# Attention weight gradients from row-form dQ, dK, dV and O: DMA transposes in the backward recurrence instead of PE transposes in the gradient stage

## The chip, the cores and the metric

The kernel runs on one core of a Trainium2 chip. The time is the device time of one execution in microseconds. The engines are PE (TensorE, matmul; its weight loads are listed as PEld), DVE (VectorE), ACT (ScalarE), POOL (GpSimd) and SP (SyncE, which only issues DMAs here). DMAs issued by SP and ACT go to hardware queues, those issued by POOL to a software queue; all of them use the core's 16 DMA engines.

## The reference, cut to what matters

A forward and its backward pass. The block is a layernorm with modulation, a recurrent memory attention (A), another layernorm, and a gated FFN (B). The attention goes through 64 segments of 32 positions; each takes 8 memory rows that the segment before has produced, so the segments must run one after the other, forward in the forward pass and backward in the backward pass.

```python
for s in range(n_seg):                       # 64 segments
    h = concatenate([mem, x[:, s*32:(s+1)*32]])        # L = 40 rows of 512
    q = einsum('btd,dhe->bhte', h, Wq)       # 32 heads of 128; k and v alike
    scores = where(mask, einsum('bhqe,bhke->bhqk', q, k) * scale, -1e9)
    p = softmax(scores)
    o = einsum('bhqk,bhke->bhqe', p, v)
    o = einsum('bhte,hed->btd', o, Wo)
    mem = o[:, :8]; outs.append(o[:, 8:])
_out, _vjp = jax.vjp(f, x, mem0, Wq, Wk, Wv, Wo, w_gate, w_up, w_down, c, w_mod)
```

The outputs are the result and the gradients of the eleven inputs. The change is about four of them: dWq, dWk, dWv (512 x 32 x 128 each) and dWo (32 x 128 x 512), which are sums over all 64 x 40 rows: dWq = sum of h(row) times dQ(row), and dWo = sum of O(row) times dA(row).

## The kernel before, in words

All phases stand in one program. A scheduler orders the instructions of each engine by their dependences and adds the semaphore waits; each engine runs its list in order. A tile pool with `bufs=n` has n buffers of a tile; whoever writes a buffer again must wait for all who use it.

**Layout.** Heads are packed three to a group of 128 columns (3 x 40 = 120 used), 11 groups used of G = 12, so a tile of one segment is 128 x 1536. In the transposed form (QT, KT, VT, OT, dQT, dKT, dVT) the partitions are the 128 features of a head and a column is head-in-group times 40 plus row. In the row form (Ost, Pst, Qst, Kst) the partitions are head-in-group times 40 plus row and the columns of a group are the 128 features.

**phase2**, forward recurrence: per segment projections, scores, softmax, P times V (which gives Ost, in row form), transposes to OT, output projection. VT, OT, Pst, Qst and Kst are stored for the backward pass, 384 KB each, from POOL. Ost has one buffer and was not stored.

**phase3**: the FFN, forward and backward, then its weight gradients, meanwhile the transposes of the attention weights.

**phase4**, backward recurrence, segments 63 to 0. `get_loads` (line 983) fetches OT, VT, Pst, Qst, Kst of the next segment on SP's queue, with two buffers each. `dot_bank` makes dOT from dyT and Wo; `ds_part` the gradient of the scores; `grad_part` (line 1052) multiplies four groups into one PSUM bank and evacuates them into dVT, dKT or dQT; `dht` multiplies these by the weights, and the fold at the end gives the memory gradient that the next segment needs in dyT. `TailRows` collects the last 8 rows of each head with a POOL copy (`dh_tail`) and works them off in pieces over the following segments. At the segment's end POOL stores dVT, dKT and dQT (lines 1116 to 1118), and the memory rows DHA. dVT has two buffers, dKT and dQT one each.

**phase5**, from line 1121: `ln_tile` does the layernorm backward of 128 positions (16 in all, spread over the gradient groups), with small loads dhb on SP and an in-between product `pr` on POOL. `build_side_rows` loads h as `hrows` and dA as `dyrows`, with the row pair of a position on 2 x 64 partitions (two rows of each of 64 segments), 20 such steps. Then 44 groups (four tensors, 11 groups of heads): load `xt` (128 features x 64 segments x 128 columns, in runs of 256 B, alternately on SP and POOL); copy it to `xr` with the segments innermost (ACT two fifths, DVE the rest); transpose it on PE, 20 steps of up to three heads (`tpg`), evacuated into `rows` by DVE and ACT; and multiply `rows` with `hrows` (`gps`, 4 x 20 matmuls of up to 384 columns, line 1252) or with `dyrows` (`gps5o`, 20 of 512 columns a head, line 1262). The results are evacuated by ACT and stored by SP. dO comes last. The program ends with the gradients of the modulation.

## Time and profile before

| | us |
|---|---|
| median of 3 runs (lowest, highest) | 4122.3 (4118.8, 4124.72) |
| the profiled execution, its own time | 4126.9 |
| its span, first to last instruction | 4125.1 |
| PE busy (share of the span) | 3714.4 (90%) |
| PEld, DVE, ACT, POOL busy | 2687.0, 1960.2, 1619.0, 749.7 |
| DMA: moved, mean rate | 603.86 MB, 146 GB/s |
| window of the forward recurrence | 50 to 1380 and on to about 1474 |
| window of the FFN weight gradients | 1930 to 2123 |
| window of the backward recurrence | 2126 to 3249 |
| window of the attention weight gradients | 3304.4 to 4090.6 |

How to read it: the page gives for each engine its busy time in the span. A matmul is pipelined, so its listed duration (323 ns on average for the 384-column ones) is longer than the step from one to the next; pace is read from unbroken runs in the timeline. A group's line has its count, busy time, mean duration, the idle time of its engine just before it, and what ended that. A DMA's issue is on its queue's engine (SPq, ACTq, POOLq), its transfer on the 16 DMA engines; a queue's line has packets, MB and the share of the 16 engines' time.

### The profile page before, as it was taken

The numbers are of one execution on the slowest core, as the hardware profiler recorded it, in microseconds if no ns is written. First come the engines' busy times: TensorE is split into PE (matmuls) and PEld (weight loads), VectorE is DVE, ScalarE is ACT, GpSimd is POOL, SyncE is SP. The second block draws the span as 40 slices with busy tenths as digits, with TensorE's granted clock in tenths as the row PEclk, the third lists the DMA queues.
The fourth block names the chain that finished last, engine by engine and source line by source line (L and its number), as shares of the span: only waits on it lengthen the run. The fifth ranks groups of instructions, "written<-read, shape, count | busy, mean of one in ns | idle before, by whom it ended". The sixth has DMA issues, their size and how long they took to land. (4 is left out here: it accounts for less than half of the span.)

```text
span 4125.1 us, 147177 instructions
## 1 busy us (share of the span) xinstructions
PE 3714.4 (90%) x66669; PEld 2687.0 (65%) x66718; DVE 1960.2 (48%) x4005; ACT 1619.0 (39%) x2984; POOL 749.7 (18%) x1191
## 2 busy tenths in 40 slices
PE   2999999999999969996989999999999579998996
PEld 2778878888888855553556666666666356665653
DVE  3444444444444447763234444444444266565454
ACT  0344443444444435541223333333333155555553
POOL 2111111111111113331111111111111121111100
PEclk6999999999999989998999999999999799999998
DMA  6222232222222243335775555555555677776773
GB/s 226 94 106 94 98 106 97 97 105 105 92 96 102 102 142 126 122 104 165 227 226 190 190 190 190 189 178 187 184 190 182 153 169 168 159 165 135 146 146 114
DMA packets 558904, 603.86 MB, mean 146 GB/s; under 512 B 367082, under 2 KB 453370, under 8 KB 556612
## 3 DMA queue, kind: packets, MB, share of 16 engines
q1 hardware_dynamic: 489220, 316.00, 28.7%
q0 software_dynamic: 61200, 264.55, 18.4%
q10 hardware_dynamic: 7856, 13.89, 1.0%
q8 instruction: 521, 8.54, 0.9%
q14 instruction: 107, 0.88, 0.1%
HBM read 319.29 MB, written 275.02 MB: 144 GB/s over the span
## 5 line engine op out<-in xcount | busy, mean ns | idle before, releaser
L1252 PE MATMUL gps<-rows,hrows 128*128 128x384 bf16 (+1 forms) x2640 | 462.2, 323 | 11.2 <-ACT ot L61 8.8
L1252 PEld LDWEIGHTS <-hrows 128*128 128x128 bf16 x2640 | 253.7, 98 | 148.4 <-issue 13.6
L63 DVE COPY rows<-tpg 128x384 bf16<-128x384 bf16 (+1 forms) x616 | 199.8, 349 | 277.7 <-PE tpg L1245 150.2
L1245 PE MATMUL tpg<-ident,xr 128*128 128x128 bf16 x2560 | 225.1, 222 | 83.5 <-ACT xr L1238 49.2
L1245 PEld LDWEIGHTS <-xr 128*128 128x128 bf16 x2560 | 183.5, 99 | 142.4 <-ACT xr L1238 49.3
L1238 ACT ACTIVATE xr<-xt 128x3072 bf16<-128x3072 bf16 (+1 forms) x44 | 235.0, 5342 | 44.5 <-DMA dhb<-DHA 43.4
L393 PE MATMUL proj_ps<-hT,Wk 128*128 128x40 bf16 x8192 | 241.4, 181 | 0.3
L393 PE MATMUL proj_ps<-hT,Wq 128*128 128x40 bf16 x8192 | 241.5, 181 | 0.0
L393 PE MATMUL proj_ps<-hT,Wv 128*128 128x40 bf16 x8192 | 231.6, 179 | 0.1
L1025 PE MATMUL proj_ps<-dyT,WoT 128*128 128x40 bf16 x8192 | 228.4, 180 | 2.3 <-DMA dyT<-DAOT 2.3
L393 PEld LDWEIGHTS <-Wk 128*128 128x128 bf16 x8192 | 229.0, 97 | 0.5 <-issue 0.4
L393 PEld LDWEIGHTS <-Wq 128*128 128x128 bf16 x8192 | 229.2, 97 | 0.0
L1025 PEld LDWEIGHTS <-WoT 128*128 128x128 bf16 x8192 | 221.8, 96 | 2.8 <-issue 2.8
L393 PEld LDWEIGHTS <-Wv 128*128 128x128 bf16 x8192 | 222.5, 96 | 0.2 <-issue 0.2
L63 DVE CAST KT<-proj_ps 128x480 bf16<-128x480 f32 (+2 forms) x256 | 119.6, 488 | 191.9 <-PE proj_ps L393 186.0
L438 ACT ACTIVATE ET<-st_ps 128x480 bf16<-128x480 f32 x192 | 109.5, 570 | 226.9 <-PE st_ps L437 226.8
L1239 DVE COPY xr<-xt 128x4608 bf16<-128x4608 bf16 (+1 forms) x44 | 176.6, 4013 | 44.1 <-DMA dhb<-DHA 44.1
L61 ACT ACTIVATE rows<-tpg 128x384 bf16<-128x384 bf16 (+1 forms) x264 | 126.7, 480 | 159.2 <-PE tpg L1245 159.1
L61 ACT ACTIVATE QT<-proj_ps 128x480 bf16<-128x480 f32 (+2 forms) x256 | 104.9, 436 | 197.9 <-PE proj_ps L393 197.9
L539 DVE TENSOR_TENSOR Pst<-tps,rden 120x512 bf16<-120x512 bf16 x192 | 131.5, 686 | 100.0 <-PE tps L405 100.0
L61 ACT ACTIVATE dVT<-g_ps 128x512 bf16<-128x512 f32 x192 | 114.6, 597 | 135.7 <-PE g_ps L1056 135.7
L61 ACT ACTIVATE dQT<-g_ps 128x512 bf16<-128x512 f32 x192 | 114.6, 597 | 113.4 <-PE g_ps L1056 113.4
(332 smaller groups left out, 7725.2 us busy)
## 6 DMA issues: line engine op xcount, KB each, us to landing
VT<-VT POOLq DMA_DIRECT2D x64, 384.0 KB, 3.0
OT<-OT POOLq DMA_DIRECT2D x64, 384.0 KB, 2.6
PS<-Pst POOLq DMA_DIRECT2D x64, 384.0 KB, 3.3
QST<-Qst POOLq DMA_DIRECT2D x64, 384.0 KB, 2.7
KST<-Kst POOLq DMA_DIRECT2D x64, 384.0 KB, 2.9
OT_l<-OT SPq DMA_DIRECT2D x64, 384.0 KB
VT_l<-VT SPq DMA_DIRECT2D x64, 384.0 KB
Pst_l<-PS SPq DMA_DIRECT2D x64, 384.0 KB
```

Of the source, the lines that this page charges most:

```text
L61: return nc.scalar.activation(out, in_, AF.Copy)
L63: return nc.vector.tensor_copy(out, in_)
L393: nc.tensor.matmul(ps[:, g_, hl * L:(hl + 1) * L], lhsT=Ws[w][:, c, h * E:(h + 1) * E], rhs=hT[:, c, :], start=(c == 0), stop=(c == DC - 1))
L438: nc.scalar.activation(part3(ET, pi)[:, :, 0:120], st_ps[:, :, 0:120], AF.Exp, scale=cfg.scale)
L539: nc.vector.tensor_tensor(part3(Pst, pi)[0:120], ps[0:120, :, :], rden[:, pi * PG:(pi + 1) * PG].unsqueeze(2).to_broadcast([120, PG, 128]) ...
L1025: nc.tensor.matmul(ps[:, g_, hl * L:(hl + 1) * L], lhsT=WoT[:, c, h * E:(h + 1) * E], rhs=dyT[:, c, :], start=(c == 0), stop=(c == DC - 1))
L1238: nc.scalar.activation(xr[:, 0:cut, :], xt[:, :, 0:cut].rearrange("p s x -> p x s"), AF.Copy)
L1239: nc.vector.tensor_copy(xr[:, cut:W, :], xt[:, :, cut:W].rearrange("p s x -> p x s"))
L1245: nc.tensor.transpose(ps[0:KR, hl, :], xr[:, c0:c0 + 2, :].rearrange("p a s -> p (a s)"), self.ident[:, :])
L1252: nc.tensor.matmul(ps[:, 0:nh * E], lhsT=hrows[0:KR, tp_, c * 128:(c + 1) * 128], rhs=rows[0:KR, tp_, 0:nh * E], start=(tp_ == 0), stop=(t ...
```

## The change

- The forward stores Ost as well, as OSR, one more POOL store a segment.
- In `grad_part`, after the evacuation of the last four groups, SP issues a DMA that transposes the tile block by block (128 x 1536 in SBUF to `rows_x`, 128 x 12 x 128 in SBUF; three buffers), and POOL stores `rows_x` as DVR, DKR or DQR. The stores of dVT, dKT, dQT at the segment's end go.
- To make room, dVT goes from two buffers to one, and the loads of Qst and Kst from two buffers to one; OT, VT and Pst keep two.
- The gradient stage has no xt, xr, tpg and no evacuation of them. Each of four tensors is cut into nine pieces (head-in-group 0, 1, 2 times the groups 0 to 3, 4 to 7, 8 to 10 or 9), loaded straight as `rows5` (2 x 64 partitions x 20 steps x up to 512 columns; runs of up to 1 KB), half on SP and half on ACT, two pieces ahead with three buffers. dWo comes first now, then dWq, dWk, dWv. The matmuls have up to 512 columns. Results are evacuated by ACT and DVE in turn and stored by POOL; since a piece holds every third head, a row's run in the dWq, dWk, dWv outputs is one head (256 B) where it was three (768 B). PSUM has four banks for them, where it had three, with three more for tpg.

```diff
@@ phase2, end of a segment
                 nc.gpsimd.dma_start(self.OT[s], gl3(OT))
+                nc.gpsimd.dma_start(self.OSR[s], gl3(Ost))
@@ phase4
+            rxp = ctx.enter_context(tc.tile_pool(name="p4rx", bufs=3))
-            dXTs = {nm: ptiles(nm, n, zero=False) for nm, n in (("dVT", 2), ("dKT", 1), ("dQT", 1))}
+            dXTs = {nm: ptiles(nm, n, zero=False) for nm, n in (("dVT", 1), ("dKT", 1), ("dQT", 1))}
-                        t = ldp.tile([128, G * GW], BF16, name=nm + "_l")
+                        t = ldp.tile([128, G * GW], BF16, name=nm + "_l", bufs=1 if nm in ("Qst", "Kst") else 2)
@@ phase4, grad_part
                     self.evac(eng, part3(xt, pi), ps[:, :, :])
+                    if pi == NP - 1:
+                        rows = rxp.tile([128, G, 128], BF16, name="rows_x")
+                        nc.sync.dma_start(rows[:], xt[:, :], transpose=True)
+                        nc.gpsimd.dma_start({"dVT": self.DVR, "dKT": self.DKR, "dQT": self.DQR}[nm][s], rows[:])
@@ phase4, end of a segment
-                nc.gpsimd.dma_start(self.DVT[s], gl3(dVT))
-                nc.gpsimd.dma_start(self.DKT[s], gl3(dKT))
-                nc.gpsimd.dma_start(self.DQT[s], gl3(dQT))
@@ phase5
-                        xt = lp.tile([128, NS, 128], BF16, name="xt")
-                        (nc.sync if li % 2 == 0 else nc.gpsimd).dma_start(xt[:], XT_dram[:, :, g, :].rearrange("s p x -> p s x"))
-                        nc.scalar.activation(xr[:, 0:cut, :], xt[:, :, 0:cut].rearrange("p s x -> p x s"), AF.Copy)
-                        nc.vector.tensor_copy(xr[:, cut:W, :], xt[:, :, cut:W].rearrange("p s x -> p x s"))
-                        for tp_ in range(NTP):
-                            ps = psT.tile([128, 3, 128], BF16, name="tpg", tag="t")
...
+                def load_rows(i):
+                    if i >= len(todo) or i in loaded:
+                        return
+                    x, _, _, (hl, g0, ng) = todo[i]
+                    t = lp.tile([128, NTP, 4 * E], BF16, name="rows5")
+                    v = x[:, hl * L:(hl + 1) * L, g0:g0 + ng, :].rearrange("s (tp tl) g e -> tl s tp (g e)", tl=2)
+                    for tl in range(2):
+                        (nc.sync, nc.scalar)[tl].dma_start(t[tl * NS:(tl + 1) * NS, :, 0:ng * E], v[tl])
+                    loaded[i] = t
...
+                for i, (_, kind, outw, (hl, g0, ng)) in enumerate(todo):
+                    load_rows(i + 2)
+                    rows = loaded.pop(i)
+                    while ln_done[0] * len(todo) < i * NT and ln_done[0] < NT:
+                        ln_step()
...
+                            self.evac(next_eng(), ot[:, 0:ng * E], ps[:, 0:ng * E])
+                            nc.gpsimd.dma_start(outw[c * 128:(c + 1) * 128, h0:h0 + 3 * (ng - 1) + 1:3, :],
+                                                ot[:, 0:ng * E].rearrange("p (h e) -> p h e", e=E))
```

The order of the instructions changes at three places on which the prediction rests. The first is SP's queue within one segment of the backward recurrence. Before, it holds the loads only (dyT is the output gradient of a later segment, the others the saved tiles):

```order
L977 DMA dyT<-DAOT 128x4x32
L988 DMA OT_l<-OT 128x1536
L988 DMA VT_l<-VT 128x1536
L988 DMA Pst_l<-PS 128x1536
L988 DMA Qst_l<-QST 128x1536
L988 DMA Kst_l<-KST 128x1536
```

The same segment of SP's queue after:

```order
L980 DMA dyT<-DAOT 128x4x32
L991 DMA OT_l<-OT 128x1536
L991 DMA VT_l<-VT 128x1536
L991 DMA Pst_l<-PS 128x1536
L991 DMA Qst_l<-QST 128x1536
L1064 DMA_TRANSPOSE rows_x<-dVT_47784 128x12x128
L991 DMA Kst_l<-KST 128x1536
L1064 DMA_TRANSPOSE rows_x<-dKT_47785 128x12x128
L1064 DMA_TRANSPOSE rows_x<-dQT_47786 128x12x128
```

The transposes of dK and dQ stand behind the load of Kst, which waits for the last matmul on the Kst before it, and ahead of the next segment's loads. The second place is POOL's list in the same stage; before, each store follows the tail copy of its tensor:

```order
L1359 COPY dh_tail_53003<-dVT_47717 128x33x8
L1116 DMA DVT<-dVT_47717 128x1536
L1359 COPY dh_tail_53004<-dKT_47718 128x33x8
L1117 DMA DKT<-dKT_47718 128x1536
L1359 COPY dh_tail_53005<-dQT_47719 128x33x8
L1118 DMA DQT<-dQT_47719 128x1536
L230 DMA DHA<-dh_rb 128x128
```

POOL's list after, one segment:

```order
L1358 COPY dh_tail_49761<-dVT_47784 128x33x8
L1358 COPY dh_tail_49762<-dKT_47785 128x33x8
L1358 COPY dh_tail_49763<-dQT_47786 128x33x8
L1065 DMA DVR<-rows_x 128x1536
L1065 DMA DKR<-rows_x 128x1536
L1065 DMA DQR<-rows_x 128x1536
L231 DMA DHA<-dh_rb 128x128
```

The stores now come behind all three copies, each of them waits for its transposing DMA, and the store of DHA is behind them. The third place is ACT in the gradient stage; before, with one group's copy, evacuations of transposes (`rows<-tpg`) and of results (`ot<-gps`):

```order
L61 ACTIVATE rows<-tpg 128x384 x6
L1238 ACTIVATE xr<-xt 128x3072
L61 ACTIVATE ot_75363<-gps_75342 128x384
L61 ACTIVATE ot_75387<-gps_75366 128x384
L61 ACTIVATE ot_75411<-gps_75390 128x384
L1336 ACTIVATE dx_tb<-xh_76302,dx_b,dx_c 128x512
L61 ACTIVATE ot_75435<-gps_75414 128x384
```

ACT after, three pieces of dWq (the rows are the new loads, DQR is dQ in row form):

```order
L61 ACTIVATE ot_76062<-gps_76041 128x512
L1236 DMA rows_76065<-DQR 64x20x512
L61 ACTIVATE ot_76159<-gps_76138 128x512
L1335 ACTIVATE dx_tb<-xh_76566,dx_b,dx_c 128x512
L61 ACTIVATE ot_76207<-gps_76186 128x512
L1236 DMA rows_76210<-DQR 64x20x512
L61 ACTIVATE ot_76258<-gps_76237 128x384
```

ACT has half of the evacuations left, and between them it issues half of each load, which waits for its buffer and for earlier DMAs.

More of the change, by code (lines that the diff above doesn't have):

```diff
@@ new lines, in phase5 @@
+                load_rows(0)
+                load_rows(1)
+                for i, (_, kind, outw, (hl, g0, ng)) in enumerate(todo):
[3 more added lines that the diff above has]
+                        ln_step()
+                    h0 = 3 * g0 + hl
+                    if kind == "qkv":
+                        for c in range(DC):
+                            ps = psG.tile([128, 4 * E], F32, name="gps5", tag="g")
+                            for tp_ in range(NTP):
+                                nc.tensor.matmul(ps[:, 0:ng * E], lhsT=hrows[:, tp_, c * 128:(c + 1) * 128],
+                                                 rhs=rows[:, tp_, 0:ng * E], start=(tp_ == 0), stop=(tp_ == NTP - 1))
+                            ot = op_.tile([128, 4 * E], BF16, name="ot5")
+                            self.evac(next_eng(), ot[:, 0:ng * E], ps[:, 0:ng * E])
+                            nc.gpsimd.dma_start(outw[c * 128:(c + 1) * 128, h0:h0 + 3 * (ng - 1) + 1:3, :],
+                                                ot[:, 0:ng * E].rearrange("p (h e) -> p h e", e=E))
+                    else:
+                        for gg in range(ng):
+                            ps = psG.tile([128, D], F32, name="gps5o", tag="g")
+                            for tp_ in range(NTP):
+                                nc.tensor.matmul(ps[:], lhsT=rows[:, tp_, gg * E:(gg + 1) * E],
+                                                 rhs=dyrows[:, tp_, :], start=(tp_ == 0), stop=(tp_ == NTP - 1))
+                            ot = op_.tile([128, D], BF16, name="ot5o")
+                            self.evac(next_eng(), ot[:], ps[:])
+                            nc.gpsimd.dma_start(outw[h0 + 3 * gg], ot[:])
```

60 lines of the change are left out of this document (12 added, 48 removed).

## The prediction

> **What bounds the kernel now.** First I asked for the busy time by stage, because the shares of the page are averages over stages. The windows are the backward recurrence, the gap behind it, the attention weight gradients and the end; the columns are PE, PEld, DVE, ACT and POOL busy, PE's granted clock, DMA share and GB/s.
>
> ```profile
> 2126.00:3249.00 1123.00, 1109.78 (x21946) 764.29 (x21942) 530.81 (x1182) 360.68 (x798) 215.07 (x464) 0.99 0.56 186
> 3249.00:3304.40 55.40, 1.59 (x10) 1.19 (x11) 7.46 (x10) 6.10 (x4) 3.40 (x3) 0.54 0.95 190
> 3304.40:4090.60 786.20, 740.03 (x5850) 478.96 (x5872) 436.83 (x851) 435.66 (x486) 110.81 (x85) 0.98 0.70 147
> 4090.60:4125.10 34.50, 0.27 (x1) 0.08 (x1) 17.96 (x17) 6.31 (x3) 0.00 (x0) 0.54 0.59 232
> ```
>
> PE bounds the recurrence (1109.8 of 1123.0 us) and the weight gradients (740.0 of 786.2 us). In the gap between them PE stands still and the DMA engines are 95% busy. Next the groups of the gradient stage:
>
> ```profile
> L1252 PE MATMUL gps<-rows,hrows 128*128 128x384 bf16 (+1 forms) x2640 | 462.2, 323 | 11.2 <-ACT ot L61 8.8 <-ACT rows L61 2.4
> L1238 ACT ACTIVATE xr<-xt 128x3072 bf16<-128x3072 bf16 (+1 forms) x44 | 235.0, 5342 | 44.5 <-DMA dhb<-DHA 43.4 <-PE tpg L1245 0.3
> L1245 PE MATMUL tpg<-ident,xr 128*128 128x128 bf16 x2560 | 225.1, 222 | 83.5 <-ACT xr L1238 49.2 <-DVE rows L63 26.5 <-ACT rows L61 6.1
> L1239 DVE COPY xr<-xt 128x4608 bf16<-128x4608 bf16 (+1 forms) x44 | 176.6, 4013 | 44.1 <-DMA dhb<-DHA 44.1
> ```
>
> The 2560 PE transposes stand on the bounding engine. The xr copies (235 us on ACT, 177 us on DVE) are big but off it, except the first, for which PE waited 49.2 us. So what counts is PE's matmuls, not the 412 us of copies that go as well.
>
> **The gradient stage.** PE's pace is read from unbroken runs in the timeline (start, length, count):
>
> ```profile
> 3702.36 4.53 PE L1252 MATMUL gps<-rows,hrows 128*128 128x256 bf16 x40 [2.92 <-ACT ot L61]
> 3711.99 11.54 PE L1252 MATMUL gps<-rows,hrows 128*128 128x384 bf16 x70
> 4062.21 1.57 PE L1245 MATMUL tpg<-ident,xr 128*128 128x128 bf16 x18
> 4066.66 11.38 PEld L1262 LDWEIGHTS <-rows 128*128 128x128 bf16 x54
> ```
>
> From first to last start, 40 matmuls of 256 columns step by 0.109 us, 70 of 384 by 0.1625 us, 54 weight loads of the 512-column matmuls by (11.38-0.10)/53 = 0.213 us, 18 transposes by about 0.08 us. After the change there are three tensors of nine pieces, each 80 matmuls; per tensor six pieces of 512, two of 384, one of 256 columns: 240 x (6x0.213 + 2x0.1625 + 0.109) = 411 us. dWo keeps 640 matmuls of 512 columns, 136 us; the layernorm sums are 32 more, 7 us. Together 554 us with no stall. A cross-check from the other side: 786 us less 2560 x 0.08 = 205 us of transposes leaves 581 us.
>
> I add 20 us of stalls, of the 46 us that PE idles there today (786.2-740.0), since waits on the layernorm loads remain: SP's queue still mixes them with the big loads, POOL now has the output stores behind the layernorm product, which waits for those loads, and evacuation needs the stored tiles free (three buffers). Behind PE four PSUM banks give some 17 us of cover (four times 20 x 0.213). Stage: 574 us, a saving of 212 us; ends 554 (saves 233) and 600 (today's whole idle time kept; saves 186).
>
> Does DMA keep up? The cost of a packet, from queue q1 in the gradient stage (3320 to 3900, 580 us, mostly 256 B packets) and in the FFN weight gradients (1935 to 2040, 105 us, mostly 896 B and 1 KB):
>
> ```profile
> q1 hardware_dynamic: 162064, 53.23, 46.3%
> q1 hardware_dynamic: 22938, 19.85, 62.3%
> ```
>
> That is 0.463x580x16/162064 = 26.5 ns, and 45.6 ns for 865 B on average. The new loads are 81,920 runs of up to 1 KB (4.1 ms at 50 ns); the dQ, dK, dV outputs become 49,152 runs of 256 B (1.3 ms); the rest about 0.8 ms: 6.2 ms over 16 engines, 390 us, under 574. The loads run two pieces ahead (36 us). ACT issues half of them between its evacuations; an issue is 0.4 to 0.6 us, but one that must wait for an earlier DMA holds the evacuations behind it, which is in the 20 us.
>
> **The gap.** First to last, SP's queue reaches the first load of a gradient group only after hrows and dyrows:
>
> ```profile
> 3258.26 2.79 POOL L1234 DMA_DIRECT2D xt<-DQT  x1 [1.91 <-issue]
> 3286.48 0.40 SPq L1234 DMA_DIRECT2D xt<-DQT  x1
> 3304.36 1.14 PE L1245 MATMUL tpg<-ident,xr 128*128 128x128 bf16 x9 [49.16 <-ACT xr L1238]
> ```
>
> The second group's load from POOL (8192 runs, 8192x26.5/16 = 13.6 us of all engines) no longer competes, and no xr copy (5.3 us) follows. Before dWo starts, hrows, dyrows and the first O piece need 6656 runs of 1 KB and 4032 of 256 B: 27.5 us of 55.4. Queue waits stay between them; I take 17 us off, ends 0 and 28.
>
> **The recurrence.** This stage is where the new work goes, and 64 segments multiply any error. Per segment three transposing DMAs of 384 KB come onto SP's queue; POOL still issues three stores of 384 KB, now of their results. PE's order is the same to the end of the stage. One segment of SP's queue, two evacuations of dV, and the DMA queues over 700 us of this stage:
>
> ```profile
> 2618.77 0.52 SPq L977 DMA_DIRECT2D dyT<-DAOT  x1
> 2619.89 0.33 SPq L988 DMA_DIRECT2D OT_l<-OT  x1
> 2620.33 0.36 SPq L988 DMA_DIRECT2D VT_l<-VT  x1
> 2622.55 0.32 SPq L988 DMA_DIRECT2D Pst_l<-PS  x1
> 2623.64 0.32 SPq L988 DMA_DIRECT2D Qst_l<-QST  x1
> 2626.06 0.32 SPq L988 DMA_DIRECT2D Kst_l<-KST  x1
> 2635.81 0.52 SPq L977 DMA_DIRECT2D dyT<-DAOT  x1
> 2622.56 0.60 ACT L61 ACTIVATE dVT<-g_ps 128x512 bf16<-128x512 f32 x1 [0.94 <-PE g_ps L1056]
> 2636.68 0.60 ACT L61 ACTIVATE dVT<-g_ps 128x512 bf16<-128x512 f32 x1 [0.40 <-PE g_ps L1056]
> q0 software_dynamic: 11200, 48.84, 17.2%
> DVT<-dVT POOLq DMA_DIRECT2D x40, 384.0 KB, 5.1
> ```
>
> No operation of this trace transposes in a DMA, so its price is bounded by two rows. As cheap as a plain 384 KB store: q0 gives 0.172x700x16/11200 = 172 ns for 4.4 KB, so 90 packets and 0.97 us of all 16 engines. Cut into runs of 128 elements, 256 B, as both sides have them: 1536 x 26.5/16 = 2.54 us. A segment is 17.04 us here (2635.81-2618.77), some 17.4 us with the tail folds; DMA is busy 56% of it, so 7.6 us are free, 2.5 us for each transpose. The cheap end costs nothing; the dear end just fills the engines, and I allow 25 us over 64 segments for it. I take the dear row, since a transpose must break lines at 128 elements, but only 8 us, since the loads run one to two segments ahead.
>
> A sentence beside that: the Trainium skill, Advanced Engine Details and Errata, X-Bar Transpose (TRN2), says that such DMAs run as fast as plain ones, 350 to 400 GB/s; by it a transpose would take an estimated 1.0 to 1.1 us and the 8 us would be zero. No trace here shows it.
>
> SP's own issue time: 2.2 us a segment today, so 14.8 us are free, 4.9 us for each transpose; the plain issues are 0.3 to 0.5 us, the dearest DMA issue of the trace 2.8 us (xt, 8192 runs). Neither binds. What now waits: the single dV buffer must be read before 2636.68, 13.5 us after its last evacuation (2623.16); dK and dQ have 12 to 14 us too. Plain stores land in 5.1 us. Single Qst and Kst are fetched as early as today (at 2623.64 and 2626.06) and needed 13 to 14 us later. On POOL the row stores wait for the transposes, and the store of DHA behind them; its buffer is written again two segments later. Each of these covers goes if a transpose takes over some 10 us to land; ACT then waits to evacuate dV and PE behind it.
>
> **The forward.** 64 more stores of 384 KB on POOL, 0.54 us of issue each, in a stage where DMA is 30% busy:
>
> ```profile
> 50.00:1380.00 1330.00, 1198.22 (x32158) 1041.37 (x32159) 581.58 (x1225) 529.78 (x1218) 225.23 (x436) 0.97 0.30 103
> ```
>
> The O rows are written anew a segment (about 20 us) later: nothing.
>
> **Sum.** -212 - 17 + 8 = -221 us. The profiled execution took 4126.9 us, 4.6 us above the median of the runs; on the median, 4122.3 - 221 = **3901 us**. The ends of the terms give 3862 and 3961.
>
> **The rivals.**
> *The transposes fill the DMA rings (slower).* Place: SP's ring, where they stand among the next segment's loads. If pieces are 128 B at the same 26.5 ns, a transpose is 3072x26.5/16 = 5.1 us, three are 15.3 us against 7.6 us free: +7.7 us a segment, +492 us, and the end is 4122 - 229 + 492 = 4385 us (229 being the two savings). It decides from (7.6 + 229/64)/3 = 3.7 us for each. For it: small packets hardly cost less than big ones, and nothing here shows the transposer. Against: whole lines are 256 B on both sides. Far beyond it lies a transposer that takes the twelve blocks one after another. The Trainium skill, VectorE: DVE Perf Modes, The three transpose paths, gives 1309 ns for one 128x128 block by DMA; if the twelve did not overlap, an estimate of 15.7 us each and 47 us a segment, about 5800 us. No row shows that either. Chance 0.19.
> *SP becomes the bound (slower).* If issuing a transpose holds SP over (14.8 + 229/64)/3 = 6.1 us, the gain is gone; at 8 us a segment is 3x8 + 2.2 = 26.2 us instead of 17.4, +563 us, 4456 us. Against: the dearest issue known is 2.8 us, and that one goes to the software queue q0. Chance 0.09.
> *The gradient stage is held by its loads.* If DMA moves no more than today's 147 GB/s there, 84 MB of rows, 17 MB of outputs and 10 MB for the layernorm take 756 us: only 30 us and the gap are gained, 4075 us. Against: 1 KB runs move 865 B in 45.6 ns, 303 GB/s. Chance 0.09.
> *Gains and losses cancel* within 0.2% (8 us, about what a measurement of this kernel tells from no change): 0.02.
>
> **How the numbers follow.** The forecast has 0.61, own range 3862 to 3961; with the held loads faster is 0.70, same 0.02, slower 0.28. Up to 4131 us that is 0.72, so the range must take in a part of the slower cases: those with transposes between 2.5 and 5.1 us end at 4385, to which I give 0.10 of the 0.28. Range 3862 to 4390.
>
> **What would show it.** Right: no tpg or xr groups; gps and gps5o in unbroken runs at 0.213 us, the gradient stage near 574 us; the recurrence still 17 us a segment, PE over 95% busy in it, DMA share up from 0.56 to between 0.7 and 1.0; the first dWo matmul some 38 us after the recurrence. Wrong: a longer segment, with ACT dVT waiting for a rows_x transpose or PE for Qst_l or Kst_l; SP without idle time between Kst_l and dyT; PE idle over 50 us in the gradients behind rows loads or ot stores.

## The result, and the profile after

The changed kernel takes 3906.7 us (median of four runs, 3903.4 to 3909.0) against 4120.6 us before (four runs, 4114.2 to 4124.7): a ratio of 0.948, 95% interval 0.947 to 0.950, or 214 us less. The prediction was 3901 us, 221 us less. The profiled execution after took 3909.0 us with a span of 3906.9 us, 218.2 us under the span before.

To see where these 218 us went, cut the span after at the same four events as before: the backward recurrence, the gap behind it, the attention weight gradients, the end. The columns are the stretch, its length, then busy time of PE, PEld, DVE, ACT and POOL, PE's granted clock, DMA share and GB/s:

```profile
2121.00:3257.00 1136.00, 1108.95 (x21952) 763.07 (x21954) 532.60 (x1182) 360.85 (x797) 223.64 (x463) 1.00 0.99 251
3257.00:3309.70 52.70, 2.27 (x25) 1.32 (x14) 2.00 (x7) 0.66 (x2) 0.64 (x2) 0.53 0.99 203
3309.70:3873.60 563.90, 562.77 (x2832) 277.64 (x2832) 125.79 (x264) 50.74 (x86) 150.97 (x203) 1.00 0.80 189
3873.60:3906.90 33.30, 0.27 (x1) 0.08 (x1) 17.91 (x17) 5.98 (x3) 0.72 (x1) 0.56 0.61 238
```

The gradient stage fell from 786.2 to 563.9 us, and PE is now busy in all but 1.1 us of it. The recurrence grew by 13 us, its PE busy time by nothing (1109.8 before, 1109.0 now), while its DMA share went from 0.56 to 0.99. The gap hardly moved, 55.4 to 52.0 us counted from PE's last product of the recurrence (3257.7), with the DMA engines as full as before. The rest is 4.6 us of an earlier start of the recurrence and 1.2 us at the end: -222.3 - 3.4 + 13.3 - 4.6 - 1.2 = -218.2 us. (The recurrence starts anywhere from 2118.0 to 2125.6 us in the kernels of this study that leave the stages ahead of it alone, so the 4.6 us are not put down to the change.)

The product groups of the gradient stage, with their idle time in the last column:

```profile
L1251 PE MATMUL gps<-rows,hrows 128*128 128x512 bf16 (+2 forms) x2160 | 417.1, 355 | 0.0
L1261 PE MATMUL gps5o<-dyrows,rows 128*128 128x512 bf16 x640 | 141.6, 384 | 45.7 <-DMA rows<-OSR 45.7
```

There are no tpg or xr groups any more, and the one wait that these groups have, 45.7 us for the first O rows, lies in the gap and not in the stage.

The recurrence is best measured by one group with a fixed place in each segment, the dO projection: its row of before, then of after, with the first and the last start (us).

```profile
L1025 PE MATMUL proj_ps<-dyT,WoT x8192: 179/179/241, 2125.5 to 3229.6; 128*128 128x40 bf16 x200
```

```profile
L1028 PE MATMUL proj_ps<-dyT,WoT x8192: 179/179/241, 2120.9 to 3238.3; 128*128 128x40 bf16 x200
```

That is 1104.1 us before and 1117.4 us after. The waits of PE in the recurrence after, by cause (total, times, longest), show where the 13 us are:

```profile
PE proj_ps L1028 <- issue: 5.6, 7, 2.5
PE dp_ps L1046 <- issue: 3.1, 2, 2.1
PE g_ps L1059 <- issue: 2.1, 1, 2.1
PE tps L1000 <- issue: 1.3, 1, 1.3
```

"Issue" is time in which PE waited for nothing that the profile shows as its releaser. There are 12.3 us of it in twelve places, up to 2.5 us each, and none in the recurrence before. No buffer, load of a tile or evacuation stands behind it. The DMA records of the same trace show what does. Queue q8, of the kind "instruction", moves 16 KB in each record. There are 170 such records in these 1117 us, one for every 255 of PE's matmuls and weight loads (256 before), so they bring PE's own instructions. All twelve waits end 1.2 to 1.6 us after such a record has landed, while the records are 6.6 us apart on average. Before, each record starts 256 of PE's instructions behind the last, with a standard deviation of 34; after, it is 255 with a deviation of 71. Some records now come late, and PE stands still until they are there.

In the gap, SP's queue and the first product behind it (start, length, engine, operation, idle time before):

```profile
3259.52 15.49 SPq L1208 DMA_DIRECT2D hrows<-AOA  x4
...
3276.45 13.77 SPq L1215 DMA_DIRECT2D dyrows<-DHA  x4
3290.27 16.38 SPq L1236 DMA_DIRECT2D rows<-OSR  x3
3309.66 15.56 PE L1261 MATMUL gps5o<-dyrows,rows 128*128 128x512 bf16 x60 [45.68 <-DMA rows<-OSR]
```

The O rows, which the first product needs, are issued on SP 33 us behind the recurrence (on ACT 30), after hrows and dyrows, and PE starts 52 us behind it.

One undisturbed segment of SP's queue after (start, length, engine, operation), and the DMA queues over the 700 us (2300 to 3000) for which the prediction showed q0 of before:

```profile
2620.73 0.54 SPq L980 DMA_DIRECT2D dyT<-DAOT  x1
...
2626.02 2.09 SPq L1064 DMA_TRANSPOSE rows_x<-dVT  x1
2628.21 0.70 SPq L991 DMA_DIRECT2D Kst_l<-KST  x1
2629.01 1.95 SPq L1064 DMA_TRANSPOSE rows_x<-dKT  x1
2631.07 2.61 SPq L1064 DMA_TRANSPOSE rows_x<-dQT  x1
2637.77 0.54 SPq L980 DMA_DIRECT2D dyT<-DAOT  x1
q1 hardware_dynamic: 234903, 126.02, 80.5%
q0 software_dynamic: 11167, 48.65, 18.5%
q8 instruction: 106, 1.74, 1.1%
```

Queue q1 over the same 700 us before:

```profile
q1 hardware_dynamic: 49920, 79.97, 38.0%
```

The segment is still 17.04 us (2637.77 - 2620.73). A transpose holds SP for 2 to 2.6 us, and SP still idles 4 us before the next dyT. Queue q1 went from 49,920 packets at 38.0% to 234,903 at 80.5%: the 120 or so transposes of this window added some 1540 packets each, the 1536 runs of 256 B that the prediction took as its dear row, and (0.805-0.380) x 700 / 120 = 2.5 us of packet time of all 16 engines each, against 2.54 forecast.

### The profile page after: what moved, and what is told of

Its sections match the earlier page's. It is cut to its first block, busy times and chain, and to the rows that moved or that the text cites. A ratio compares the mean times of both kernels' runs of the same rounds, so it can differ in the third digit from the quotient of the medians.

```text
span 3906.9 us, 140933 instructions
## 1 busy us (share of the span) xinstructions
PE 3536.1 (91%) x63678; PEld 2483.0 (64%) x63678; DVE 1645.7 (42%) x3415; ACT 1228.9 (31%) x2582; POOL 832.9 (21%) x1373
## 4 chain that ended last, share of the span: by engine, by line
PE 80%; DVE 7%; DMA 5%; issue 4%; ACT 2%; SPq 1%; POOL 0%; DVEq 0%; POOLq 0%; ACTq 0%
PE proj_ps L394 15%; PE gps L1251 11%; PE dh_ps L208 9%; PE proj_ps L1028 5%; PE tps L406 5%; PE g_ps L1059 4%; PE at_ps L208 3%; PE gps5o L1261 3%; PE gps L843 3%; PE mm L757 2%; PE tps L1000 2%; PE dh_tps L208 2%; DVE Ost L459 2%; PE dh_ft L219 2%; PE at_ft L219 2%
## 5 line engine op out<-in xcount | busy, mean ns | idle before, releaser
L1251 PE MATMUL gps<-rows,hrows 128*128 128x512 bf16 (+2 forms) x2160 | 417.1, 355 | 0.0
L1251 PEld LDWEIGHTS <-hrows 128*128 128x128 bf16 x2160 | 211.5, 98 | 204.1
L63 DVE CAST ot<-gps 128x512 bf16<-128x512 f32 (+3 forms) x77 | 48.7, 634 | 369.5 <-PE gps L1251 198.1
L1261 PE MATMUL gps5o<-dyrows,rows 128*128 128x512 bf16 x640 | 141.6, 384 | 45.7 <-DMA rows<-OSR 45.7
L521 POOL DMA_DIRECT2D VT<-VT x64 | 34.9, 545 | 679.2 <-ACT VT L61 631.4
L61 ACT ACTIVATE ot<-gps 128x512 bf16<-128x512 f32 (+3 forms) x77 | 42.4, 551 | 397.8 <-PE gps L1251 232.4
L208 PE MATMUL dh_ps<-WvT,dVT 128*32 128x512 bf16 x2048 | 145.9, 383 | 0.0
L63 DVE CAST dKT<-g_ps 128x512 bf16<-128x512 f32 x192 | 131.8, 687 | 29.0 <-PE g_ps L1059 28.3
```

Source lines behind the costliest of these rows:

```text
L61: return nc.scalar.activation(out, in_, AF.Copy)
L63: return nc.vector.tensor_copy(out, in_)
L208: self.nc.tensor.matmul(ps[32 * j:32 * j + 32, :], lhsT=lhsT, rhs=w, start=(n < 4), stop=(n >= total - 4), tile_position=(0, 32 * j))
L1251: nc.tensor.matmul(ps[:, 0:ng * E], lhsT=hrows[:, tp_, c * 128:(c + 1) * 128], rhs=rows[:, tp_, 0:ng * E], start=(tp_ == 0), stop=(tp_ == ...
L1261: nc.tensor.matmul(ps[:], lhsT=rows[:, tp_, gg * E:(gg + 1) * E], rhs=dyrows[:, tp_, :], start=(tp_ == 0), stop=(tp_ == NTP - 1))
```

## The experiments

The first question is what the transposing DMAs cost in the recurrence (plain_copy, extra_third, dram3, dram3b, alone); the second what held the gap (early_o, early_o2); the third what the gradient stage really gained (dummy_tpg, w384). The last runs put together what was found.

**plain_copy: the same DMAs without transposing.** The stored rows are then not transposed, so the weight gradients of Q, K and V hold other numbers.

```diff
-                        nc.sync.dma_start(rows[:], xt[:, :], transpose=True)
+                        nc.sync.dma_start(rows[:], gl3(xt))
```

> The three transposing DMAs of a segment become plain DMAs of the same 384 KB between the same tiles; the rows stored for dQ, dK and dV are then not transposed, so out_3 to out_5 hold other numbers, at the same instructions elsewhere. Theory 1: the 13 us that the recurrence lost (1104.1 to 1117.4 us from the first to the last dO projection) come from the transposes' load on the DMA rings, and reach PE as waits of 1 to 2.5 us put down to issue (12.3 us in all). Then the recurrence comes back to 1103 to 1107 us, those waits fall under 2 us, the DMA share of the stage falls from 0.99 to between 0.65 and 0.8 (0.56 and three copies at about 0.97 us), and the time is 3892 to 3897 us. Rival: the waits come from something else in the new order (single dV, Q and K buffers, stores that wait on POOL): the recurrence stays at 1115 to 1119 us and the time at 3905 to 3909 us.

Measured: 3899.6 us (0.946 of before, 0.944 to 0.948). The recurrence went from 2125.6 to 3229.5, 1103.9 us, the length of before. Its stage, and all that is left of PE's issue waits in it:

```profile
2119.00:3257.00 1138.00, 1115.10 (x21988) 766.74 (x21986) 533.49 (x1191) 362.11 (x800) 226.89 (x468) 0.99 0.74 252
PE proj_ps L1028 <- issue: 0.5, 1, 0.5
PE dp_ps L1046 <- issue: 0.3, 1, 0.3
```

Theory 1 holds: single buffers, the stores behind POOL's copies and the 384 KB per tensor are all still there, and only the transposing made the 13 us. (It is the transposing as a whole: this edit does not tell the transposing itself from the cutting into 1536 packets.) The instruction records are nearer to even again, with a deviation of 47. The forecast of the time, 3892 to 3897 us, was missed: the median fell by 7 us. In the profiled execution the recurrence started 4.7 us later than in that of the changed kernel, and the edit touches nothing ahead of it.

**extra_third: 512 more columns transposed in each segment.**

```diff
+                        if nm == "dVT":
+                            extra = rxp.tile([128, 4, 128], BF16, name="rows_y", bufs=1)
+                            nc.sync.dma_start(extra[:], xt[:, 0:4 * 128], transpose=True)
```

> One more transposing DMA in each segment, of a third of the dV tile (4 of 12 blocks) into a tile that nobody reads: an estimated 0.83 us of all 16 DMA engines, and some 2 us of SP's queue, which idles about 4 us a segment. Theory 1: the DMA share of 0.99 means that the rings are full and nothing is left, so a segment grows by 0.83 us, the recurrence by 53 us to about 1170 us, the time to about 3960 us. Rival: the share counts packets that wait, and the rings still have slack because the loads run a segment or more ahead: the recurrence grows by 0 to 8 us, the time stays at 3905 to 3915 us. Under both SP does not become the bound.

Measured: 3912.4 us (0.949, 0.947 to 0.950); the recurrence 2123.1 to 3241.3, 1118.2 us, 0.8 us more than without. The window and the waits:

```profile
2119.00:3257.00 1138.00, 1109.28 (x21905) 762.42 (x21907) 533.28 (x1184) 360.85 (x797) 225.18 (x465) 0.99 1.07 258
PE proj_ps L1028 <- issue: 8.9, 11, 2.4
```

The DMA share in the last column but one is 1.07. A share over 1 can't be occupancy: the packets of one engine overlap in this count. So 0.99 did not mean full, and theory 1 of this run is refuted: an estimated 0.83 us of packet time more in each segment (1.4 us by the two shares) cost 0.8 us in all 64 together. That is less than the 5 us by which the recurrence differs between the runs with unchanged transposes (1113.8 to 1118.8 us).

**dram3 and dram3b: how much room is left.** Three plain copies of 1536 runs of 240 B are added to each segment. In dram3 they were made from a tensor that was ready early:

```diff
+                        nc.sync.dma_start(self.SCR[s, :, :, 0:120], self.QST[s, :, :, 0:120])
```

> Behind each transposing DMA of a segment SP also issues a plain copy of the segment's Q rows within DRAM, 1536 runs of 240 B, into a tensor that nobody reads; no SBUF and no wait is added, and some 1.5 us of SP's 4 idle us. Each is about as many packets as a transpose. Theory 1: the DMA share of 0.99 to 1.07 counts packets that overlap, and the engines still have room: so three more such groups make the recurrence 5 to 60 us longer through later landings and PE's waits for instructions, 3912 to 3970 us. Rival A: a transpose costs the 2.5 us of all engines that its packets' time gives, and after it the engines are just full: +7 us a segment, +450 us, about 4360 us. Rival B: a transpose costs about 1 us, so that some 4 us a segment are left: +3.5 us a segment, +220 us, about 4130 us.

This run missed its aim. The row of the copies gives their first and last issue, 130 to 1672 us: they ran during the forward, not in the recurrence, which stayed at 1118.8 us. The total, one run of 3986 us, is 79 us more, because the recurrence starts 76 us later (2197.3 against 2120.9); it says nothing about the question.

```profile
L1066 SPq DMA_DIRECT2D SCR<-QST x192: 469/470/1908, 130.2 to 1672.2; - x192
```

So the copies were made to depend on a row store of the segment before:

```diff
+                        if s < NS - 1:
+                            prev = {"dVT": self.DVR, "dKT": self.DKR, "dQT": self.DQR}[nm]
+                            nc.sync.dma_start(self.SCR[s, :, :, 0:120], prev[s + 1, :, :, 0:120])
```

> The same three extra copies a segment, now surely within the recurrence: each reads the row tensor that the segment before stored, 1536 runs of 240 B, and writes a DRAM tensor that nobody reads (in the run before, the copies were issued during the forward, where they depended on nothing later, and said nothing of the recurrence). Theory 1: the DMA share of 0.99 counts packets that overlap or stand in the ring, and the engines have room: the recurrence grows from 1117 us by 5 to 60 us. Rival A: the 2.5 us of packet time are what a transpose takes from all engines, and they are just full: +7 us a segment, +450 us. Rival B: a transpose really takes about 1 us, some 4 us a segment are left: +3.5 us a segment, +220 us.

Measured: 4281 us in one run, slower than before. The recurrence, and what PE waited for in it:

```profile
L1029 PE MATMUL proj_ps<-dyT,WoT x8192: 179/179/241, 2122.5 to 3602.9; 128*128 128x40 bf16 x200
...
PE g_ps L1060 <- DMA Qst_l<-QST: 177.8, 53, 6.6
PE dh_ps L209 <- ACT dVT L61: 62.6, 46, 2.9
```

In the same run ACT waited 167 us before evacuating dV, over part of the recurrence alone:

```profile
ACT dVT L61 <- DMA rows_x<-dVT: 167.0, 31, 7.8
```

The recurrence is 1480.4 us, 363 us or 5.7 us a segment longer, between the two rivals and far above theory 1. At first sight it looks as the prediction's list of wrong signs put it: PE waits for Qst_l, ACT for the transposing DMA that reads the single dV buffer. But SP's own waits show that the edit did something else as well (the waits over the whole recurrence, then three lines of SP's queue):

```profile
SPq L1068 <- DMA SCR<-DVR: 266.3, 62, 7.3
SPq L1068 <- DMA DVR<-rows_x: 95.0, 55, 5.3
...
2617.74 0.48 SPq L1068 DMA_DIRECT2D SCR<-DVR  x1
...
2625.07 0.48 SPq L1068 DMA_DIRECT2D SCR<-DKR  x1
...
2627.47 3.83 SPq L1065 DMA_TRANSPOSE rows_x<-dVT  x1
```

The three copies of a segment write the same part of SCR, so SP waits until one has landed before it issues the next, and for the first it waits for a row store. That held SP's queue for 361 us, about as much as the recurrence grew. Behind them stood the loads of the next segment and the transposing DMA of dV: its tile was complete at 2616.1, and it was issued at 2627.5, 11 us later (in the changed kernel's segment above, 0.9 us later). The transposes also took longer to land, 6.2 us in the median against 4.4. And 115 of the 363 us are PE's own products (1205.6 us busy against 1090.8), at a granted clock of 0.90 in place of 1.00; the other 248 us are waits. So this run does not separate a queue that is blocked from engines that are full, and it gives no figure for the room that was left. What is shown is the lower end: extra_third's third of a transpose, 0.6 to 0.8 us of a 17.7 us segment, was free.

**alone: the price by itself.** Behind all the work, twelve transposes of 128x1536, then twelve plain DMAs of the same size.

```diff
+            tsrc = wp.tile([128, 12 * 128], BF16, name="tsrc")
+            nc.vector.tensor_copy(tsrc[:], dmod_bc[:, 0:12 * 128])
...
+            for i in range(12):
+                nc.sync.dma_start(tdst[i][:], tsrc[:, :], transpose=True)
+            for i in reversed(range(12)):
+                nc.sync.dma_start(pdst[i][:], tdst[i][:])
```

> The price by itself: at the end of the program, where little else moves, twelve transposing DMAs of 128x1536 from one tile into twelve tiles, then twelve plain DMAs of the same size from these. The output is untouched; the end grows by what they take. Theory 1: a transpose takes 2.4 to 2.6 us of all engines, as its 1536 packets do in the recurrence, so the twelve take 29 to 32 us while nothing else moves, and the plain ones 0.9 to 1.1 us each, 11 to 13 us. Rival: packets in the recurrence are drawn out by the others beside them, and a transpose alone takes 1.0 to 1.5 us, so the twelve take 12 to 18 us, unless SP's issue of each (2.3 to 2.7 us in the recurrence) is a cost of its own, which would show as engines idle between them.

SP's queue, and the DMA engines in 10 us where only transposes run (3900 to 3910):

```profile
3887.31 24.76 SPq L1283 DMA_TRANSPOSE tdst<-tsrc  x12
3912.18 10.92 SPq L1285 DMA_DIRECT2D pdst<-tdst  x12
...
DMA packets 8377, 2.10 MB, mean 210 GB/s; under 512 B 8377, under 2 KB 8377, under 8 KB 8377
q1 hardware_dynamic: 8377, 2.10, 111.9%
```

And in 5 us where only the plain ones run (3915 to 3920):

```profile
DMA packets 726, 1.98 MB, mean 397 GB/s; under 512 B 80, under 2 KB 80, under 8 KB 726
```

Both expectations for the transpose were off. 8377 packets in 10 us are 5.45 transposes of 1536: 1.83 us for each with all engines in use, and the share of 111.9% shows again that packet time counts 12% or more too much. A plain 384 KB DMA takes 0.393 MB / 397 GB/s = 0.99 us. So a transpose costs 1.85 plain ones, between the two ends of the prediction (0.97 and 2.54 us). SP issued each in 24.76 / 12 = 2.06 us even here (1.82 in the median), against medians of 2.3 to 2.7 us in the recurrence, so most of that time is not due to contention there. This is one run (3939.3 us), and the price of a transpose among other DMAs was not measured.

**early_o: dWo's loads ahead of the others.**

```diff
-                hrows = build_side_rows(self.H1ROWS, "hrows", mem_h)
-                dyrows = build_side_rows(self.DAROWS, "dyrows", mem_dy)
...
                 load_rows(0)
+                dyrows = build_side_rows(self.DAROWS, "dyrows", mem_dy)
+                hrows = build_side_rows(self.H1ROWS, "hrows", mem_h)
                 load_rows(1)
```

> Only the order of the loads behind the recurrence changes: the first O piece, then dyrows, then hrows, then the second piece. Theory 1: the first dWo matmul came 52 us after the recurrence (17 us later than forecast) because both queues work through hrows first and the rings also carry pieces two and three; dWo needs only dyrows and the first piece, 5 MB, 25 us at the 203 GB/s of this gap, and some us of landing. So the gap falls to 28 to 34 us, nothing comes back later (hrows are needed 140 us later), and the time is 3885 to 3890 us. Rival: what holds the gap is the issue of the eight small loads of DHA rows (13.8 us for four on SP), which stay ahead of the first matmul, and the rings share themselves out among all that is queued: the gap stays over 42 us, the time over 3896 us.

Measured: 3903.9 us (0.947, 0.946 to 0.949), 3 us less than the changed kernel, not 20. The start of dWo on PE; its recurrence ended at 3256.9:

```profile
3278.58 1.44 PE L1261 MATMUL gps5o<-dyrows,rows 128*128 128x512 bf16 x3 [16.20 <-DMA dyrows<-DHA]
...
3288.20 17.31 PE L1261 MATMUL gps5o<-dyrows,rows 128*128 128x512 bf16 x75 [0.53 <-DMA dyrows<-DHA]
3321.03 4.13 PE L1261 MATMUL gps5o<-dyrows,rows 128*128 128x512 bf16 x11 [15.52 <-DMA rows<-OSR]
```

The products run from 3288.2, 31 us behind the recurrence, as theory 1 said. What it overlooked is the second piece: hrows stood ahead of it in the queues, and PE waited 15.5 us for it. The rival was right in part: what PE waits for in these 31 us is dyrows from DHA, the small loads of memory rows (16.2, 6.6 and 0.5 us), and the issue of the four on each queue takes 11.7 us on SP and 12.2 us on ACT.

**early_o2: hrows last.** As before, with `load_rows(1)` and `load_rows(2)` ahead of hrows.

> The order of the loads behind the recurrence again: first O piece, dyrows, second and third O piece, and hrows last. Where hrows came between dyrows and the second piece, PE started 21 us earlier but then waited 15.5 us for the second piece. Theory 1: the rings take about 10 us for a piece of 2.5 MB and 15 us for hrows, in the order of issue, and dWo needs one piece in 17 us; so with hrows last no wait comes back: first dWo matmul as early as there, all of dyrows there some 31 us after the recurrence, no wait over 3 us for O rows or hrows, and 3884 to 3890 us. Rival: the queues stand still for another reason (small loads of 252 rows hold a queue whatever the rings carry), so the second piece is late again or hrows delay piece four: 10 us or more of waits in the O pieces, 3895 to 3904 us.

Measured: 3901.2 us (0.947, 0.946 to 0.949). The gap and the stage behind it:

```profile
3261.80:3295.40 33.60, 4.08 (x18) 1.68 (x16) 2.00 (x7) 0.66 (x2) 0.64 (x2) 0.55 1.00 232
3295.40:3868.20 572.80, 565.64 (x2827) 277.53 (x2827) 127.27 (x264) 50.70 (x86) 150.55 (x203) 0.99 0.81 191
...
PE acc_ps L1164 <- DMA dhb<-DHB: 4.2, 1, 4.2
PE acc_ps L1167 <- POOL pr L1166: 1.7, 2, 1.2
PE acc_ps L1164 <- DMA dhb<-DHA: 1.1, 1, 1.1
```

The gap is 33.6 us, 18 less than in the changed kernel, and no O piece is waited for any more: the order of the queues was the cause of these 18 us. But 6 of the 18 us come back as waits for layernorm loads (7.0 us where the changed kernel had 1.0), which now arrive later than PE, and the stage as a whole is 9 us longer. From the recurrence's end to the last product's start are 605.9 us against 615.5, so 10 us are left, and the median shows 5.5. The time forecast for theory 1, 3884 to 3890 us, was wrong, its mechanism right.

**dummy_tpg: the 2560 PE transposes put back,** with results that nobody reads.

```diff
+                    for tp_ in range(NTP):
+                        tp = psG.tile([128, 4, E], BF16, name="tpg", tag="t", bufs=2)
+                        for gg in range(ng):
+                            nc.tensor.transpose(tp[:, gg, :], rows[:, tp_, gg * E:(gg + 1) * E], self.ident[:, :])
```

> The 2560 PE transposes of 128x128 that the change took from the gradient stage are put back, with results that nobody reads and no copies behind them. Theory 1: the saving of that stage (786.2 to 563.9 us) is mostly the transposes' own time on the bounding PE, 2560 x 0.08 = 205 us, and the waits that went are the rest. Then the stage is 760 to 775 us and the time 4105 to 4115 us. Rival: most of the saving came from wider matmuls and the waits for evacuations, copies and loads (46 us idle, 83.5 us put down to tpg), and transposes run for the most part beside the weight loads: the stage grows by 100 to 150 us, and the time is 4010 to 4060 us.

Measured: 4062.5 us (0.985, 0.984 to 0.987), 156 us over the changed kernel. The group:

```profile
L1249 PE MATMUL tpg<-ident,rows 128*128 128x128 bf16 x2560 | 157.4, 219 | 45.1 <-DMA rows<-OSR 45.1
```

In the profiled executions the stage grew by 148 us, from 563.9 to 711.8 us (the medians differ by 156 us). A transpose in unbroken blocks of 40 to 80 thus costs 0.058 to 0.061 us (148 or 156 us over 2560), not the 0.08 us read from a run of 18 before. The growth of the stage is in the rival's range, the time 2.5 us above it. So the transposes in their cheapest form are 148 to 156 of the 222 us; before, PE idled 45 us more in this stage (46.2 against 1.1 us), and 21 to 29 us are left.

**w384: pieces of three heads instead of four.**

```diff
-                chunks = [(hl, g0, min(4, (H - hl + 2) // 3 - g0)) for hl in range(3) for g0 in (0, 4, 8)]
+                chunks = [(hl, g0, min(3, (H - hl + 2) // 3 - g0)) for hl in range(3) for g0 in (0, 3, 6, 9)]
```

> Pieces of at most three heads (384 columns) in place of four in the gradient stage, 12 pieces of each tensor where there were nine; all else as in the changed kernel. The stage saved 222 us: 46 us of PE's idle time, and 177 us of PE's busy time, of which the transposes put back gave 156 us. Theory 1: the 21 us left are the width, fewer and wider matmuls and weight loads: the stage grows by 15 to 25 us, the time is 3922 to 3932 us. Rival: by the paces read from unbroken runs (0.1625 us for 384 columns, 0.213 us for 512) the width is worth only 7 us (418 against 411 us), 3910 to 3917 us, and the rest was lost at each change between transposes and products.

Measured: 3910.2 us (0.950, 0.948 to 0.952), 3.5 us more.

```profile
L1251 PE MATMUL gps<-rows,hrows 128*128 128x384 bf16 (+2 forms) x2880 | 419.6, 308 | 4.2 <-DVE ot L63 3.6 <-ACT ot L61 0.6
```

The products take 2.5 us more (419.6 against 417.1) and 4.2 us of waits for evacuations appear, 6.7 us together: the rival's 7 us. (The gap was 3 us shorter in this profile, 48.8 us against 52.0.) So the width of the pieces is 6 to 7 of the 21 to 29 us. By elimination the rest belongs to the old interleaving of short groups of transposes with products; no run here took that apart.

**g11_early2: a faster version.** The order of early_o2, and the transposing DMAs and row stores move 11 of the 12 blocks, since the twelfth is padding.

```diff
-                        rows = rxp.tile([128, G, 128], BF16, name="rows_x")
-                        nc.sync.dma_start(rows[:], xt[:, :], transpose=True)
+                        rows = rxp.tile([128, 11, 128], BF16, name="rows_x")
+                        nc.sync.dma_start(rows[:], xt[:, 0:11 * 128], transpose=True)
-                        nc.gpsimd.dma_start({"dVT": self.DVR, "dKT": self.DKR, "dQT": self.DQR}[nm][s], rows[:])
+                        nc.gpsimd.dma_start({"dVT": self.DVR, "dKT": self.DKR, "dQT": self.DQR}[nm][s, :, 0:11, :], rows[:])
```

> The same order of loads, and the transposing DMAs and row stores move 11 of the 12 blocks (the twelfth is padding that no later step reads). Theory 1 (PE's waits for instructions in the recurrence come from the packets of the transposes, and all 1536 of each gone took 12 us off): an eighth to a twelfth less of them takes 1 us off at most, so the time is 0 to 2 us below that of the same order alone. Rival: the waits start only above a threshold of load, and 8% less falls below it: 8 to 12 us less.

Measured: 3895.6 us (0.946, 0.945 to 0.949); the recurrence 1110.9 us, where the kernels with the transposes of the change as they are had 1113.8 to 1118.8. Its interval overlapped with that of the changed kernel, so both were run again on one chip:

> The changed kernel once more, so that the next kernel is compared with it on the same chip in the same rounds: 3903 to 3909 us by every theory.

> The eleven blocks with the new order of loads once more. In its first run the recurrence was 1110.9 us (1117.4 in the changed kernel) and 609 us lay between the recurrence's end and the last product (616), 13 us in all, against 11 us in the medians, whose intervals overlap. Theory: the gain is real, 3893 to 3898 us. Rival: half of it is the spread between runs, 3899 to 3904 us.

Measured: the changed kernel 3910.9 us (0.9489 of before, 0.9475 to 0.9503), this one 3891.8 us (0.9447, 0.9429 to 0.9464). The intervals no longer overlap: 19 us less than the change alone. In the two profiles the recurrence is 1109.7 us against 1117.5, and from its end to the last product are 602 us against 615. PE's waits for issue in the recurrence are 4.2 us, against 9.7:

```profile
PE proj_ps L1028 <- issue: 2.9, 4, 1.3
PE dp_ps L1050 <- issue: 1.0, 1, 1.0
PE dp_ps L1046 <- issue: 0.3, 1, 0.3
```

In both runs the recurrence is shorter than in every kernel with the full transposes, by 3 to 9 us, where a twelfth of the 13 us would be 1.1. So theory 1's "1 us at most" falls. The rival's 8 to 12 us were not reached, and no threshold was measured. The waits for issue alone show less: 7.4 us in the first run and 4.2 in the second, against 7.6 to 12.3 us with the full transposes. The row stores carry a twelfth less too, which these runs do not separate.

## Why the prediction was right, step by step

**What bounds it.** Right. PE's matmuls were what counted, not the 412 us of xr copies: PE's busy time in the gradient stage fell by 177 us, and the stage by 222.

**The gradient stage.** Forecast 574 us, measured 563.9. The sum of what stays was the good one: 554 us from the paces of 512, 384 and 256 columns, against 562.8 us busy. Of the 20 us of stalls 1.1 came: four banks and three row buffers covered the stores and ACT's loads. So the sum was 9 us too low and the stalls 19 us too high. The cross-check by what goes was weaker than it looked: 2560 x 0.08 = 205 us, where a transpose put back costs 0.058 to 0.061 us, 148 to 156 us in all. It came out near only because 45 us of waits and the interleaving went as well. Held loads, the third rival, did not show: the stage moves 189 GB/s with PE busy throughout. The count of loads against it was a little low: nine pieces of four tensors at 2560 runs are 92,160 runs, not 81,920, since the shorter pieces have as many; at the same 50 ns that is 32 us more of all engines, 422 us, still under the 574.

**The gap.** This term was mis-sized: 17 us forecast, 3.4 measured. The step that failed is that the second group's load from POOL "no longer competes": it is gone, but as many bytes came in its place. The engines moved 10.5 MB in the gap before (190 GB/s over 55.4 us) and 10.7 MB after (203 GB/s over 52.7 us, at a share of 0.99); where two groups of 2.1 MB stood in the queues, three O pieces, 7.2 MB, stand now. And the first O piece, like the first groups before, is issued last, behind hrows that PE needs 140 us later. With hrows moved back (early_o2) the gap was 18 us shorter. The count of 27.5 us was too low as well. It took in hrows, dyrows and the first O piece. Without hrows it is 17.7 us at the same prices, and in that order the products ran 31 to 34 us behind the recurrence (early_o, early_o2), waiting for the small DHA loads.

**The recurrence.** Forecast +8 us, measured +13, in the range of 0 to 25. The structure held: segments of 17 us, 1540 packets for each transpose, SP not the bound, every cover long enough. Two readings in it were wrong. The first is the price of a transpose: alone it is 1.83 us of all engines and not 2.54. Packet time over-counts 12% there, which is 0.2 us of the difference; the rest is that a packet takes 21 ns alone (111.9% of 10 us of 16 engines over 8377) and 26 ns in the recurrence (2.5 us of 16 engines over 1536). The second is the mechanism: I gave the loss to landings that come late. It came instead as PE's waits for its own instructions, whose records start late while the transposes are there. With plain copies these waits all but go (0.8 us, plain_copy). What holds a record up on its way is not shown.

**The sum.** The three terms missed by 10, 14 and 5 us: 222 us saved in the stage where 212 were forecast, 3.4 in the gap for 17, 13 lost in the recurrence for 8. Together they are -212 us for -221, and another 6 us came from an earlier start and a shorter end that nobody forecast. That the medians differ by 214 us, 7 from the forecast, is in part luck.

By the Trainium skill, Advanced Engine Details and Errata, X-Bar Transpose (TRN2), such DMAs are as fast as plain ones, 350 to 400 GB/s; here the transposes ran at 210 GB/s alone and the plain ones at 397, so the measurement decides against that sentence for this shape.

**The rivals.** "The transposes fill the DMA rings" decided, in the prediction, from 3.7 us each; with 1.83 us alone, and 2.5 us of packet time in the recurrence, it did not happen. In dram3b the waits that were named for it did come, and the gain became a loss (4281 us), but there the added copies held SP's queue, so it does not show full engines. The page behind its far end, the Trainium skill's VectorE: DVE Perf Modes, The three transpose paths, has 1309 ns for one 128x128 block; here a DMA of twelve blocks takes 1.83 us, so they do not follow one another at that price. "SP becomes the bound" decided from 6.1 us of issue each; it was 2 to 2.6.

**The forward.** Forecast nothing for 64 more stores; its end moved by no more than it does between runs (its last projection starts at 1471.0 us here, at 1469.9 to 1476.5 in other runs with the same forward, at 1474.1 before).

## What to carry to other kernels

When work leaves the bounding engine, sum up what stays on it, at the pace of unbroken runs; a price for what goes, taken from short bursts, mixes in the cost of switching. When a stage begins behind a burst of loads, put them in the order of first use, all of them: a piece moved to the front is worth only as much as the next one behind it allows. And a DMA share near 1.0 is not a verdict: add a small and then a larger load to the stage, and see which one lengthens it, but look that the added load does not itself hold up a queue that the stage needs, as it did in dram3b.

## What the hardware showed that I had not expected

- A DMA share above 1 (1.07 in extra_third, 111.9% of one queue in alone): packet times overlap, so packet time over-counts what short packets take.
- A transposing DMA of 128x1536 bf16 between SBUF tiles takes 1.83 us of all 16 engines (210 GB/s) against 0.99 us for a plain one, and holds SP's queue for 2.06 us (1.82 in the median) with little else moving.
- PE lost 0.2 to 2.5 us at a time to "issue" while transposes ran (12.3 us in the recurrence; 0.8 us with plain copies in their place). All of these waits end 1.2 to 1.6 us after a 16 KB record of queue q8, "instruction", has landed; one such record comes for every 255 instructions of PE, and its start becomes uneven (a deviation of 71 instructions, 34 before).
